# Chunked attention with a fused feed-forward layer: g, the second queries and the first tiles in another order

## The chip, the cores and the metric

The kernel runs on one core of a Trainium2 chip. The metric is the device time of one execution in microseconds (us); a kernel's time is the median of several executions. The profile comes from one more execution, taken by the hardware profiler. TensorE (PE) multiplies matrices, VectorE (DVE) and ScalarE (ACT) work element by element, GpSimd (POOL) and SyncE (SP) mainly issue transfers (DMAs) here; POOL also does some small arithmetic.

## The reference

Attention in chunks, with a few memory keys and values for each head, and then a feed-forward layer on the result:

```python
B, H, S, D = 4, 8, 768, 64        # chunk 32, left context 16, right context 8, 8 memory keys
for c in range(S // 32):
    q_c = q[:, :, 32*c : 32*c + 32]
    k_ctx, v_ctx = k, v at positions max(0, 32*c - 16) to min(S, 32*c + 40)
    k_full, v_full = concat(mem_k, k_ctx), concat(mem_v, v_ctx)
    a = softmax(q_c @ k_full.T / sqrt(D))
    attn[:, :, 32*c : 32*c + 32] = a @ v_full
x  = attn.transpose(0, 2, 1, 3).reshape(B, S, 512)
xn = (x - mean(x)) / sqrt(var(x) + 1e-6) * g_ln
out = x + max(xn @ w_ch1, 0) @ w_ch2          # w_ch1 512 x 2048, w_ch2 2048 x 512
```

All inputs and the output are float32; the kernel multiplies in float16.

## The kernel before

**Tiles, groups and blocks.** A tile is 128 rows of the sequence of one batch entry; there are six for each of four entries, 24 in all. A group is 64 rows (two chunks) and has its own window of 104 key columns in `KT`: 16 keys to its left, 64 own, 8 to its right, 8 zero columns and 8 memory keys. Tile t works with groups 2t and 2t+1. A block is 256 rows, so four groups or two tiles: queries and keys are loaded a block at a time.

**From load to output.** Keys and queries arrive in `st` (the very first blocks in float32, in output buffers borrowed for it), are rearranged by a copy into `iv` (`mix`, `mix_raw`), turned by TensorE against an identity matrix (`transpose_block`, `first_q`), and copied from PSUM into `KT` (`window`, `pieces`, `key_left`, `key_right`) and `QR` (`part_q`, `whole_q`). For a tile, `scores` (line 289) makes 16 products into an `att` slot of PSUM, `soften` two exponentials on ACT, `values` (line 312) 16 products with `V` and then a reciprocal, a scaling and a mean on DVE; `norm` (line 335) subtracts the mean and multiplies by g, which `gb` holds on all 128 partitions; `turn_x` (line 356) turns the result into `xT`. The feed-forward layer takes W1 in four quarters `w1c` and W2 in four `w2c`. `up_tile(u, c, i)` (line 398) multiplies tile i of a group of three with quarter c of W1 (16 products) and clips below zero with `relu` into `rT`; `up` does the same for three tiles at once; `down` multiplies with W2 and adds up in PSUM, and `finish` scales, adds x and stores. V also needs rows for the memory values (`v_mem`), which come from `mem_v` by `mem_vals`.

**What sets the order.** The order is written out by hand, and each engine runs its own instructions in that order, waiting for what it needs. Lines 560 to 629 are the start: tiles 0 to 2 of the first batch entry, and the first up tiles, all written call by call. From line 630 on a plan (`at(u, step, ...)`) places calls beside steps of the feed-forward layer: u counts groups of three tiles, and in the first group steps 10 to 15 are the last six `up_tile` calls, from step 16 on `down`. PSUM has two `att` slots and four `mm` banks, each taken in turn by `slot`; one is free again when its reader on DVE or ACT is done. `warm(n)` (line 455) issues n products of a zero matrix with 512 columns that nobody reads.

**The transfers.** SP's queue loads the first keys and queries and small tensors (lines 469 to 485); POOL's queue (lines 510 to 552, then the plan) loads everything else in the order written, converting to float16 on the way. A transfer on POOL's queue is issued when the eighth one before it has landed.

**g before.** `moe_g_ln` is loaded into one row, `grow`; `spread_g` (line 556) multiplies it on TensorE with a row of ones, `gone`, in two halves, into the bank `mm[3]`, and DVE copies that to `gb` (line 585).

**The first 30 us as written.** After key block 0 and the first half of query block 0 come tile 0's scores, then the second query half with the second half of g, tile 0's values, the turn of key block 1 and ACT's copies of it with the right edge of group 3 (lines 591 to 594), tile 1's scores, first up tiles, the turn of the whole query block 1 (lines 611 to 613), tile 2's scores, and further up tiles. DVE's `mix(0, 2, 0)` (line 626) prepares key block 2, which `turn_keys` turns in step 12.

Of the kernel before, what the change touches and what calls it, by code (L numbers as in the profile page):

```python
# [8 lines left out]
FP32 = mybir.dt.float32  # L9
# [6 lines left out]
def kernel(  # L16
# [34 lines left out]
    memv16 = sb.tile([W, B, H, VW], FP16, name="memv16")  # L51
    memKT = sb.tile([128, B, 4, 8], FP16, name="memKT")
    gb = sb.tile([128, 512], FP32, name="gb")
    grow = sb.tile([1, 512], FP32, name="grow")
    gone = sb.tile([1, 128], FP32, name="gone")
    band = sb.tile([128, 2], FP32, name="band")
    cnt = sb.tile([128, 3], FP32, name="cnt")
    mhalf = sb.tile([128, 1], FP32, name="mhalf")
# [31 lines left out]
    def dram(t, offset, pattern):  # L90
        return bass.AP(tensor=t.tensor, offset=offset, ap=[list(p) for p in pattern])
# [17 lines left out]
    def pick(lst, key):  # L109
        key = (id(lst),) + key  # L110
        if key not in ring:
            ring[key] = ring.setdefault(("n", id(lst)), 0) % len(lst)
            ring[("n", id(lst))] += 1
        return lst[ring[key]]


    def load_block(b, blk, which):
        s = pick(st, ("b", b, blk, which))
        for par in range(2):
            nc.gpsimd.dma_start(  # L120
                out=s[:, 512 * par : 512 * par + 512],
                in_=dram((k, q)[which], (b * H + 4 * par) * HS + blk * 256 * D,
                         [[512, 32], [HS, 4], [1, 512]]),
            )

    def load_v(b, g):
        lo, hi = 16 if g == 0 else 0, 80 if g == NG - 1 else 96
        nc.gpsimd.dma_start(  # L128
            out=V[b % 2][lo:hi, g, :, 0:64],
            in_=dram(v, b * H * HS + (64 * g - 16 + lo) * D, [[64, hi - lo], [HS, H], [1, 64]]),  # L130
        )

    def v_mem(b, g0, g1, eng):
        src = memv16[96:W, b, :, :]
        copy(eng, free(V[b % 2][96:W, g0:g1, :, :], 0, [[H * VW, g1 - g0], [1, H * VW]]),
             bass.AP(tensor=src.tensor, offset=src.offset,
                     ap=[list(src.ap[0]), [0, g1 - g0], [1, H * VW]]))

    def load_w1(c):
        nc.gpsimd.dma_start(  # L140
            out=w1c[c], in_=dram(moe_w_ch1, 512 * c, [[FF, 128], [128 * FF, 4], [1, 512]])
        )
# [54 lines left out]
    def pieces(b, blk, banks, phase):  # L197

        for n in range(2):
            key_piece(b, banks[phase], 4 * blk + n, *PIECES[n], dve, phase)  # L200
            key_piece(b, banks[1 - phase], 4 * blk + 2 + n, *PIECES[2 + n], act, 1 - phase)

    def window(b, blk, banks, k0, eng):

        for half in ((0, 1) if eng is dve else (1, 0)):
            key_piece(b, banks[half], 4 * blk + k0, *PIECES[k0], eng, half)
# [45 lines left out]
    def mix_raw(which, srcs, half, eng, lo=0, hi=128):  # L252

        o = pick(iv, ("b", 0, 0, which))[lo:hi, :]
        r0, n = (0, 8) if half is None else (4 * half, 4)
        for par in range(2):
            copy(eng, free(o, 128 * r0 + 64 * par, [[128, n], [1, 64]]),
                 free(srcs[par][lo:hi, :], 64 * r0, [[64, n], [1, 64]]))

    def first_q(half):  # L260

        i = pick(iv, ("b", 0, 0, 1))
        rows = slice(64 * half, 64 * half + 64)
        for r in range(8):
            c = 128 * r + 64 * half
            nc.tensor.matmul(
                out=Q0[0][:, c : c + 64],
                lhsT=i[rows, 128 * r : 128 * r + 128], rhs=identity[rows, rows],
                is_transpose=True, start=True, stop=True, tile_position=(64 * half, 0),
            )  # L270

    def mix(b, blk, which, eng):
        s, o = pick(st, ("b", b, blk, which)), pick(iv, ("b", b, blk, which))
        copy(eng, free(o, 0, [[64, 2], [128, 8], [1, 64]]), s)
# [29 lines left out]
    def soften(b, t, c):  # L304
        p = score_slot[b, t]
        nc.scalar.activation(  # L306
            out=free(AT[t % 3], 32 * c, [[64, 16], [1, 32]]),
            in_=free(p, 4 * c, [[64, 16], [1, 4], [8, 8]], W),
            func=ACTF.Exp, bias=band[0:W, c : c + 1], scale=0.125,
        )  # L310
# [152 lines left out]
    def first_load(which, par, lo, hi, eng):  # L463
        eng.dma_start(
            out=raws[which][par][4 * lo : 4 * hi, :],
            in_=dram((k, q)[which], 4 * par * HS + 512 * lo, [[512, hi - lo], [HS, 4], [1, 512]]),
        )
# [3 lines left out]
    nc.sync.dma_start(out=memkf, in_=dram(mem_k, 0, [[512, 32], [1, 512]]))  # L471
    first_load(1, 0, 0, 16, nc.sync)
    first_load(1, 1, 0, 16, nc.gpsimd)
    nc.sync.dma_start(out=grow, in_=dram(moe_g_ln, 0, [[512, 1], [1, 512]]))

    nc.sync.dma_start(out=xs[5][96:W, :], in_=dram(mem_v, 0, [[64, 8], [512, 8], [1, 64]]))

    def load_mem_v():
        nc.gpsimd.dma_start(
            out=memv16[96:W, 1:B, :, 0:64].rearrange("p b h d -> p (b h) d"),  # L480
            in_=dram(mem_v, 4096, [[64, 8], [512, 24], [1, 64]]),
        )

    first_load(1, 0, 16, 32, nc.sync)
    first_load(1, 1, 16, 32, nc.sync)

    PAIR = 1.0 / 128 + 15.0 / 2**20

# [20 lines left out]
    ones(0, 0, 2, pool)  # L509
    load_block(0, 1, 0)  # L510
    nc.vector.memset(zero, 0.0)
    nc.vector.memset(gone, 1.0)
    clear_keys(0, dve)
    nc.vector.memset(mhalf, -0.5)
    nc.vector.memset(memv16.bitcast(FP32)[96:W, :, :, 32:40], PAIR)
# [11 lines left out]
    load_w1(0)  # L527
    load_v(0, 2)
    load_v(0, 3)
    load_w1(1)  # L530
    load_block(0, 1, 1)
    load_w1(2)
    load_v(0, 4)
    load_v(0, 5)
    load_w1(3)
    load_block(0, 2, 0)
    nc.gpsimd.memset(V[0][64:96, NG - 1, :, :], 0.0)
# [15 lines left out]

    K0 = [as16(mm[0]), as16(mm[1])]
    Q0 = [as16(mm[2]), as16(mm[3])]
    def spread_g(half):
        cols = slice(256 * half, 256 * half + 256)
        nc.tensor.matmul(out=mm[3][:, cols], lhsT=gone, rhs=grow[:, cols], start=True, stop=True)

    warm(10)  # L560
    mix_raw(0, raws[0], 0, dve)
    mix_raw(0, raws[0], 1, act)
# [3 lines left out]
    mem_keys()  # L566
    mix_raw(1, raws[1], 0, dve, 0, 64)
    mix_raw(1, raws[1], 1, act, 0, 64)
    first_q(0)
    window(0, 0, K0, 0, dve)  # L570
    window(0, 0, K0, 1, act)
    part_q(0, 0, 0, Q0[0], act)
    spread_g(0)
    memT()
    mem_cols(0, dve)
    scores(0, 0)
    mem_vals()
    soften(0, 0, 0)
    soften(0, 0, 1)
    mix_raw(1, raws[1], None, dve, 64, 128)  # L580
    v_mem(0, 0, 2, dve)
    mix(0, 1, 0, dve)
    spread_g(1)
    first_q(1)
    copy(dve, gb, mm[3])
    part_q(0, 0, 1, Q0[0], dve)
    values(0, 0)
    norm(0, 0)
    window(0, 0, K0, 2, act)
    window(0, 0, K0, 3, act)  # L590
    transpose_block(0, 1, 0, Q0)
    window(0, 1, Q0, 0, act)
    window(0, 1, Q0, 1, act)
    key_right(0, 3, act)
    warm(3, 512, mm[1])
    scores(0, 1)
    soften(0, 1, 0)
    soften(0, 1, 1)
    turn_x(0, 0)
    v_mem(0, 2, 4, dve)  # L600
    window(0, 1, Q0, 2, dve)
    window(0, 1, Q0, 3, act)
    key_left(0, 4, dve)
    turn["mm"] = 3
    up_tile(0, 0, 0, act)
    mix(0, 1, 1, act)
    values(0, 1)
    norm(0, 1)
    late = up_tile(0, 1, 0, None)
    turn_x(0, 1)  # L610
    Q1 = [as16(slot("mm")) for _ in range(2)]
    transpose_block(0, 1, 1, Q1)
    whole_q(0, 1, Q1)
    scores(0, 2)
    soften(0, 2, 0)
    soften(0, 2, 1)
    relu(dve, *late)
    v_mem(0, 4, 6, dve)
    up_tile(0, 0, 1, act)
    up_tile(0, 1, 1, dve)  # L620
    values(0, 2)
    norm(0, 2)
    up_tile(0, 2, 0, act)
    up_tile(0, 2, 1, act)
    turn_x(0, 2)
    mix(0, 2, 0, dve)
    total(cnt[:, 1:2], 0, 80)
    total(cnt[:, 2:3], 96, W)
# [7 lines left out]
    def attend(i, s0, s1, u):  # L636
# [11 lines left out]
        else:  # L648
            at(i // 3 - 1, (20, 22, 23)[i % 3], root, b, t)

    def root0(b, t):
        root(0, t)

    at(0, 12, turn_keys, 0, 2)
    at(0, 12, more_keys, 0, 2)
    at(0, 14, mix, 0, 2, 1, dve)
# [124 lines left out]
```

## Time and profile before

| | us |
|---|---|
| median of 8 runs | 224.27 |
| lowest and highest | 223.04, 224.83 |
| the profiled execution's own time | 224.55 |
| its span, first to last instruction | 222.8 |
| TensorE busy in it | 213.1 (96%) |
| VectorE, ScalarE, GpSimd busy | 134.5, 102.9, 99.0 |

Four views of the profile are used. The 40 slices show, for each engine, the busy share of a slice in tenths (9 is 90% or more); PEclk is the share of TensorE's clock that was granted, in tenths, and DMA the busy share of the 16 DMA engines. A table of stretches gives busy microseconds of PE, PEld (weight loads), DVE, ACT and POOL, with the number of instructions in brackets, then the granted clock, the DMA share and GB/s. The waits say which instruction's line waited for which, with the total in us, the count and the longest. A row of the timeline has the start, the duration, the engine, the line, the operation and what it writes and reads, and in brackets the idle time ahead of it and what ended that. L12 is line 12 of the kernel. Products are pipelined, so their durations can overlap.

### The profile page before, as it was taken

How to read it: one execution, taken by the hardware profiler on the slowest of the kernel's cores; microseconds unless marked ns; L12 is line 12 of the kernel's file. 1: busy time of each engine (PE TensorE's matmuls, PEld its weight loads, DVE VectorE, ACT ScalarE, POOL GpSimd, SP SyncE). 2: the span in 40 equal slices, each digit the busy share in tenths (PEclk: the TensorE clock that was granted, in tenths of full speed). 3: DMA queues.
4: the chain of work that ended last, by engine and by line, in shares of the span. 5: the costliest groups of instructions: out<-in, count | busy, mean ns of one | idle time of the engine just before them, and what ended most of it. 6: DMA issues, size and time to landing. Idle time of an engine off the chain costs nothing.

```text
span 222.8 us, 5004 instructions
## 1 busy us (share of the span) xinstructions
PE 213.1 (96%) x1974; PEld 131.6 (59%) x1974; DVE 134.5 (60%) x329; ACT 102.9 (46%) x217; POOL 99.0 (44%) x171
## 2 busy tenths in 40 slices
PE   7786979999999999999999999999999999999993
PEld 2566977547765566546664567446654666456553
DVE  4868456588879768834675678716845367234221
ACT  2755449525784246732791067424851365103200
POOL 7955695899598992212923793300021011100000
PEclk9759699999999999999999999999999999999999
DMA  6999999999969999277995799585112201211012
GB/s 167 185 193 193 199 194 204 171 143 192 163 98 165 172 183 164 46 165 188 133 161 93 101 159 183 59 192 129 26 24 74 94 15 35 71 57 40 0 47 94
DMA packets 72273, 27.70 MB, mean 124 GB/s; under 512 B 60345, under 2 KB 68281, under 8 KB 72250
## 3 DMA queue, kind: packets, MB, share of 16 engines
q0 software_dynamic: 46080, 14.71, 63.2%
q1 hardware_dynamic: 26026, 12.41, 24.3%
q8 instruction: 15, 0.25, 0.4%
q10 hardware_dynamic: 144, 0.26, 0.4%
q14 instruction: 8, 0.07, 0.1%
HBM read 30.28 MB, written 6.29 MB: 164 GB/s over the span
## 4 chain that ended last, share of the span: by engine, by line
PE 79%; DMA 13%; POOL 5%; issue 1%; DVE 0%; DVEq 0%; POOLq 0%
PE mm L420 34%; PE mm L391 34%; DMA w1c<-in_moe_w_ch_dram 8%; PE att L296 5%; DMA st<-in_k_dram 5%; PE att L317 3%; POOL V L128 2%; PE mm L442 2%; POOL w2c L145 1%; POOL st L120 1%; PE att L218 1%; PE mm L218 1%; POOL V L491 0%; PE att L365 0%; POOL V L548 0%
## 5 line engine op out<-in xcount | busy, mean ns | idle before, releaser
L420 PE MATMUL mm<-w2c,rT 128*128 128x512 f16 x368 | 83.0, 379 | 0.0
L391 PE MATMUL mm<-xT,w1c 128*128 128x384 f16 x448 | 78.5, 327 | 0.0
L391 PEld LDWEIGHTS <-w1c 128*128 128x128 f16 x448 | 49.1, 114 | 22.1
L420 PEld LDWEIGHTS <-rT 128*128 128x128 f16 x368 | 34.9, 98 | 39.4
L385 DVE TENSOR_SCALAR rT<-mm 128x384 f16<-128x384 f32 (+1 forms) x61 | 34.3, 567 | 26.9 <-PE mm L391 21.7
L383 ACT ACTIVATE rT<-mm 128x384 f16<-128x384 f32 (+1 forms) x63 | 31.6, 506 | 40.8 <-PE mm L391 23.4
L306 ACT ACTIVATE AT<-att,band 104x512 f16<-104x512 f32 x48 | 31.3, 686 | 29.3 <-PE att L296 29.3
L128 POOL DMA_DIRECT2D V<-in_v_dram x48 | 39.5, 834 | 5.9 <-DMA w1c<-in_moe_w_ch_dram 3.9
L429 DVE SCALAR_TENSOR_TENSOR osb<-mm,rstd,xs 128x512 f32<-128x512 f32 x23 | 17.2, 749 | 33.6 <-PE mm L420 24.7
L348 POOL TENSOR_SCALAR veps<-sq 128x1 f32<-128x1 f32 x24 | 7.4, 309 | 66.3 <-ACT junk L342 52.8
L342 ACT ACTIVATE junk<-xs,nmean 128x512 f16<-128x512 f32 x24 | 17.4, 726 | 15.1 <-DVE nmean L331 13.2
L337 DVE SCALAR_TENSOR_TENSOR xn<-xs,nmean,gb 128x512 f16<-128x512 f32 x24 | 18.0, 748 | 0.4
L296 PE MATMUL att<-QR,KT 64*104 64x64 f16 x384 | 16.0, 235 | 1.2 <-ACT QR L102 1.1
L325 DVE SCALAR_TENSOR_TENSOR xs<-att,rec 128x512 f32<-128x512 f32 x24 | 16.6, 692 | 0.8
L296 PEld LDWEIGHTS <-KT 64*104 64x104 f16 x384 | 12.9, 135 | 5.7 <-issue 3.8
L352 POOL TENSOR_TENSOR rstd<-veps,mhalf 128x1 f32<-128x1 f32 x24 | 14.6, 610 | 2.0
L402 PE MATMUL mm<-xT,w1c 128*128 128x128 f16 x192 | 13.3, 233 | 1.5 <-DVE xT L370 1.5
L120 POOL DMA_DIRECT2D st<-in_k_dram x22 | 13.4, 639 | 2.0 <-DVE KT L104 2.0
L120 POOL DMA_DIRECT2D st<-in_q_dram x22 | 12.6, 595 | 3.0 <-DMA w2c<-in_moe_w_ch_dram 1.9
L402 PEld LDWEIGHTS <-w1c 128*128 128x128 f16 x192 | 12.3, 119 | 2.1 <-DVE xT L370 1.2
L317 PEld LDWEIGHTS <-AT 104*64 104x64 f16 x384 | 8.4, 114 | 7.3 <-issue 4.3
L102 ACT COPY KT<-rawk 128x352 f16<-128x352 f16 (+1 forms) x12 | 9.0, 814 | 5.7 <-DMA rawk<-iv 5.7
(78 smaller groups left out, 141.4 us busy)
## 6 DMA issues: line engine op xcount, KB each, us to landing
out_dram<-osb SPq DMA_DIRECT2D x23, 256.0 KB, 2.2
V<-in_v_dram POOLq DMA_DIRECT2D x40, 96.0 KB, 5.2
st<-in_k_dram POOLq DMA_DIRECT2D x22, 128.0 KB, 5.2
st<-in_q_dram POOLq DMA_DIRECT2D x22, 128.0 KB, 6.5
w1c<-in_moe_w_ch_dram POOLq DMA_DIRECT2D x4, 512.0 KB, 10.0
w2c<-in_moe_w_ch_dram POOLq DMA_DIRECT2D x4, 512.0 KB, 8.6
V<-in_v_dram POOLq DMA_DIRECT2D x8, 80.0 KB, 5.5
xT<-xn SPq DMA_TRANSPOSE x17, 2.4
```

The source lines that it names most:

```text
L120: nc.gpsimd.dma_start(out=s[:, 512 * par : 512 * par + 512], in_=dram((k, q)[which], (b * H + 4 * par) * HS + blk * 256 * D, [[512, 32], [ ...
L128: nc.gpsimd.dma_start(out=V[b % 2][lo:hi, g, :, 0:64], in_=dram(v, b * H * HS + (64 * g - 16 + lo) * D, [[64, hi - lo], [HS, H], [1, 64]]),)
L296: nc.tensor.matmul(out=p[0:W, par, (4 * gg + j) * 64 : (4 * gg + j) * 64 + 64], lhsT=KT[b % 2][rows, 2 * t + gg, j, :], rhs=free(QR[b % 2] ...
L306: nc.scalar.activation(out=free(AT[t % 3], 32 * c, [[64, 16], [1, 32]]), in_=free(p, 4 * c, [[64, 16], [1, 4], [8, 8]], W), func=ACTF.Exp, ...
L337: nc.vector.scalar_tensor_tensor(out=xn[i % 4], in0=xs[i % 9], scalar=nmean[t], in1=gb, op0=ALU.add, op1=ALU.mult,)
L342: nc.scalar.activation(out=junk, in_=xs[(NT * b + t) % 9], func=ACTF.Square, bias=nmean[t], scale=1.0, accum_out=sq[t],)
L383: nc.scalar.activation(out=o, in_=p, func=ACTF.Relu)
L385: nc.vector.tensor_scalar(out=o, in0=p, scalar1=0.0, scalar2=None, op0=ALU.max)
L391: nc.tensor.matmul(out=p, lhsT=free(w1c[c][:, dt, :], i, [[4, 128]]), rhs=xT[u % 2][:, dt, 128 * lo : 128 * (lo + n)], start=(dt == 0), st ...
L402: nc.tensor.matmul(out=p[:, 128 * k_ : 128 * k_ + 128], lhsT=free(w1c[c][:, dt, :], k_, [[4, 128]]), rhs=xT[u % 2][:, dt, 128 * i : 128 * ...
L420: nc.tensor.matmul(out=p, lhsT=rT[c][:, k_, 128 * i : 128 * i + 128], rhs=w2c[c][:, k_, :], start=(c == 0 and k_ == 0), stop=(c == 3 and k ...
L429: nc.vector.scalar_tensor_tensor(out=o, in0=p, scalar=rstd[t % 9], in1=xs[t % 9], op0=ALU.mult, op1=ALU.add,)
```

## The change

Three things change, and with them the order of the start.

- g comes to all 128 partitions by one transfer on SP's queue that reads the same row for each; `grow`, `gone`, `spread_g` and the copy fall away. The second half of the first queries is moved ahead of `mem_v` and g on that queue.
- Query block 1 is loaded, rearranged and turned in two halves of 64 partitions (`load_q`, `mix_q`, `half_q`). The half for tile 2 is loaded ahead of W1's quarter 1, and V's groups 4 and 5 ahead of quarter 2; the half for tile 3 is loaded ahead of quarter 3 and turned in step 11 of the plan (`late_q`).
- Key block 1 is turned ahead of tile 0's values. For tile 1's scores only its first eight keys are copied (`first_right`, on DVE); the other copies of block 1 follow tile 1's values.

More fillers (`warm`) stand between the calls: 13 in place of 3 after the first query half. Two up tiles change places, and some copies change engine. In the diff below, context is cut.

```diff
     memv16 = sb.tile([W, B, H, VW], FP16, name="memv16")
     memKT = sb.tile([128, B, 4, 8], FP16, name="memKT")
     gb = sb.tile([128, 512], FP32, name="gb")
-    grow = sb.tile([1, 512], FP32, name="grow")
-    gone = sb.tile([1, 128], FP32, name="gone")
     band = sb.tile([128, 2], FP32, name="band")
     cnt = sb.tile([128, 3], FP32, name="cnt")
     mhalf = sb.tile([128, 1], FP32, name="mhalf")
...
             key_piece(b, banks[phase], 4 * blk + n, *PIECES[n], dve, phase)
             key_piece(b, banks[1 - phase], 4 * blk + 2 + n, *PIECES[2 + n], act, 1 - phase)
 
+    def first_right(b, g, banks):
+
+        for half in range(2):
+            copy(dve, free(KT[b % 2], GW * g + 80 + 4 * half, [[W, 4], [1, 4]]),
+                 free(banks[half], 0, [[1, 4], [128, 4]]))
+
     def window(b, blk, banks, k0, eng):
 
         for half in ((0, 1) if eng is dve else (1, 0)):
...
             copy(eng, free(o, 128 * r0 + 64 * par, [[128, n], [1, 64]]),
                  free(srcs[par][lo:hi, :], 64 * r0, [[64, n], [1, 64]]))
 
-    def first_q(half):
-
-        i = pick(iv, ("b", 0, 0, 1))
+    def load_q(b, blk, half):
+        s = pick(st, ("b", b, blk, 1))[64 * half : 64 * half + 64, :]
+        for par in range(2):
+            nc.gpsimd.dma_start(
+                out=s[:, 512 * par : 512 * par + 512],
+                in_=dram(q, (b * H + 4 * par) * HS + (blk * 256 + 128 * half) * D,
+                         [[512, 16], [HS, 4], [1, 512]]),
+            )
+
+    def mix_q(b, blk, half, eng):
+        rows = slice(64 * half, 64 * half + 64)
+        s, o = pick(st, ("b", b, blk, 1))[rows, :], pick(iv, ("b", b, blk, 1))[rows, :]
+        copy(eng, free(o, 0, [[64, 2], [128, 8], [1, 64]]), s)
+
+    def half_q(b, blk, half, pv):
+
+        i = pick(iv, ("b", b, blk, 1))
         rows = slice(64 * half, 64 * half + 64)
         for r in range(8):
             c = 128 * r + 64 * half
             nc.tensor.matmul(
-                out=Q0[0][:, c : c + 64],
+                out=pv[:, c : c + 64],
                 lhsT=i[rows, 128 * r : 128 * r + 128], rhs=identity[rows, rows],
                 is_transpose=True, start=True, stop=True, tile_position=(64 * half, 0),
             )
...
     nc.sync.dma_start(out=memkf, in_=dram(mem_k, 0, [[512, 32], [1, 512]]))
     first_load(1, 0, 0, 16, nc.sync)
     first_load(1, 1, 0, 16, nc.gpsimd)
-    nc.sync.dma_start(out=grow, in_=dram(moe_g_ln, 0, [[512, 1], [1, 512]]))
-
+    first_load(1, 0, 16, 32, nc.sync)
+    first_load(1, 1, 16, 32, nc.sync)
     nc.sync.dma_start(out=xs[5][96:W, :], in_=dram(mem_v, 0, [[64, 8], [512, 8], [1, 64]]))
+    nc.sync.dma_start(out=gb, in_=dram(moe_g_ln, 0, [[0, 128], [1, 512]]))
 
     def load_mem_v():
         nc.gpsimd.dma_start(
             out=memv16[96:W, 1:B, :, 0:64].rearrange("p b h d -> p (b h) d"),
             in_=dram(mem_v, 4096, [[64, 8], [512, 24], [1, 64]]),
         )
-
-    first_load(1, 0, 16, 32, nc.sync)
-    first_load(1, 1, 16, 32, nc.sync)
 
     PAIR = 1.0 / 128 + 15.0 / 2**20
 
...
     ones(0, 0, 2, pool)
     load_block(0, 1, 0)
     nc.vector.memset(zero, 0.0)
-    nc.vector.memset(gone, 1.0)
     clear_keys(0, dve)
     nc.vector.memset(mhalf, -0.5)
     nc.vector.memset(memv16.bitcast(FP32)[96:W, :, :, 32:40], PAIR)
...
     load_w1(0)
     load_v(0, 2)
     load_v(0, 3)
+    load_q(0, 1, 0)
     load_w1(1)
-    load_block(0, 1, 1)
-    load_w1(2)
     load_v(0, 4)
     load_v(0, 5)
+    load_w1(2)
+    load_q(0, 1, 1)
     load_w1(3)
     load_block(0, 2, 0)
     nc.gpsimd.memset(V[0][64:96, NG - 1, :, :], 0.0)
...
 
     K0 = [as16(mm[0]), as16(mm[1])]
     Q0 = [as16(mm[2]), as16(mm[3])]
-    def spread_g(half):
-        cols = slice(256 * half, 256 * half + 256)
-        nc.tensor.matmul(out=mm[3][:, cols], lhsT=gone, rhs=grow[:, cols], start=True, stop=True)
-
     warm(10)
     mix_raw(0, raws[0], 0, dve)
     mix_raw(0, raws[0], 1, act)
...
     mem_keys()
     mix_raw(1, raws[1], 0, dve, 0, 64)
     mix_raw(1, raws[1], 1, act, 0, 64)
-    first_q(0)
+    half_q(0, 0, 0, Q0[0])
     window(0, 0, K0, 0, dve)
     window(0, 0, K0, 1, act)
     part_q(0, 0, 0, Q0[0], act)
-    spread_g(0)
+    warm(3)
     memT()
     mem_cols(0, dve)
     scores(0, 0)
     mem_vals()
     soften(0, 0, 0)
     soften(0, 0, 1)
+    mix(0, 1, 0, dve)
+    transpose_block(0, 1, 0, Q0)
+    v_mem(0, 0, 2, dve)
     mix_raw(1, raws[1], None, dve, 64, 128)
-    v_mem(0, 0, 2, dve)
-    mix(0, 1, 0, dve)
-    spread_g(1)
-    first_q(1)
-    copy(dve, gb, mm[3])
-    part_q(0, 0, 1, Q0[0], dve)
+    warm(2, 512, att[1][:, 0, :])
+    half_q(0, 0, 1, as16(att[1][:, 1, :]))
+    first_right(0, 3, Q0)
+    part_q(0, 0, 1, as16(att[1][:, 1, :]), dve)
+    v_mem(0, 2, 4, dve)
     values(0, 0)
     norm(0, 0)
     window(0, 0, K0, 2, act)
     window(0, 0, K0, 3, act)
-    transpose_block(0, 1, 0, Q0)
-    window(0, 1, Q0, 0, act)
-    window(0, 1, Q0, 1, act)
-    key_right(0, 3, act)
-    warm(3, 512, mm[1])
+    warm(2, 512, att[0][:, 1, :])
     scores(0, 1)
     soften(0, 1, 0)
     soften(0, 1, 1)
+    warm(4, 512, mm[1])
     turn_x(0, 0)
-    v_mem(0, 2, 4, dve)
+    values(0, 1)
+    norm(0, 1)
+    window(0, 1, Q0, 0, act)
+    window(0, 1, Q0, 1, act)
+    key_left(0, 4, dve)
+    turn["mm"] = 3
+    late = up_tile(0, 0, 0, None)
+    mix_q(0, 1, 0, act)
+    warm(2, 512, mm[1])
+    Q1 = as16(slot("mm"))
+    half_q(0, 1, 0, Q1)
+    part_q(0, 1, 0, Q1, act)
     window(0, 1, Q0, 2, dve)
     window(0, 1, Q0, 3, act)
-    key_left(0, 4, dve)
-    turn["mm"] = 3
-    up_tile(0, 0, 0, act)
-    mix(0, 1, 1, act)
-    values(0, 1)
-    norm(0, 1)
-    late = up_tile(0, 1, 0, None)
     turn_x(0, 1)
-    Q1 = [as16(slot("mm")) for _ in range(2)]
-    transpose_block(0, 1, 1, Q1)
-    whole_q(0, 1, Q1)
     scores(0, 2)
     soften(0, 2, 0)
     soften(0, 2, 1)
     relu(dve, *late)
     v_mem(0, 4, 6, dve)
+    up_tile(0, 1, 0, act)
     up_tile(0, 0, 1, act)
-    up_tile(0, 1, 1, dve)
     values(0, 2)
     norm(0, 2)
+    up_tile(0, 1, 1, act)
     up_tile(0, 2, 0, act)
+    turn_x(0, 2)
     up_tile(0, 2, 1, act)
-    turn_x(0, 2)
+    mix_q(0, 1, 1, dve)
     mix(0, 2, 0, dve)
     total(cnt[:, 1:2], 0, 80)
     total(cnt[:, 2:3], 96, W)
...
         else:
             at(i // 3 - 1, (20, 22, 23)[i % 3], root, b, t)
 
+    def late_q():
+        pv = as16(slot("att")[:, 0, :])
+        half_q(0, 1, 1, pv)
+        part_q(0, 1, 1, pv, act)
+
     def root0(b, t):
         root(0, t)
 
+    at(0, 11, late_q)
     at(0, 12, turn_keys, 0, 2)
     at(0, 12, more_keys, 0, 2)
     at(0, 14, mix, 0, 2, 1, dve)
```

## The prediction

> **What bounds the kernel now.** I read the page first, its 40 slices.
>
> ```profile
> PE   7786979999999999999999999999999999999993
> ...
> PEclk9759699999999999999999999999999999999999
> DMA  6999999999969999277995799585112201211012
> ```
>
> A slice is 5.6 us. From the seventh on TensorE is full to the end, so what is saved there is only what TensorE need not do. Ahead of it, in the first 30 us, it has gaps and a lowered clock, and the DMA engines are full from the second slice. The change touches this start only, so I asked for a table of stretches, cut where the granted clock changes (every 3.41 us).
>
> ```profile
> 5.41:8.82 3.41, 2.39 (x36) 1.41 (x35) 3.01 (x10) 2.18 (x7) 3.41 (x6) 1.00 1.43 190
> 8.82:12.24 3.42, 3.12 (x42) 2.41 (x43) 2.92 (x7) 2.92 (x8) 2.90 (x4) 0.50 1.40 176
> 12.24:15.65 3.41, 3.26 (x31) 2.11 (x30) 1.93 (x6) 1.04 (x6) 1.78 (x3) 0.50 1.55 199
> 15.65:19.06 3.41, 2.74 (x52) 2.35 (x50) 2.65 (x9) 2.56 (x6) 1.39 (x3) 1.00 1.24 201
> 19.06:22.48 3.42, 1.80 (x35) 1.68 (x36) 2.76 (x6) 1.56 (x3) 2.40 (x5) 1.00 1.67 187
> 22.48:25.89 3.41, 3.41 (x45) 3.19 (x42) 0.43 (x1) 1.59 (x3) 1.44 (x3) 0.50 1.58 189
> 25.89:29.30 3.41, 2.42 (x41) 2.05 (x36) 2.33 (x7) 1.19 (x2) 3.33 (x6) 1.00 1.22 207
> ```
>
> After the length come busy us of PE, weight loads, DVE, ACT and POOL, then the clock. The idle stretch 19.06:22.48 (PE 1.80) is followed by one at half clock that is packed with up tiles: those cost 1.7 us more than at full clock. Next, who made TensorE wait (4 to 40 us), and the timeline rows around it.
>
> ```profile
> PE mm L402 <- DVE xT L370: 1.5, 2, 1.0
> PE att L296 <- ACT QR L102: 1.1, 2, 0.7
> PE att L365 <- DVE xn L337: 1.1, 1, 1.1
> ```
>
> ```profile
> 20.00 0.40 PE L365 MATMUL att<-identity,xn 128*128 128x128 f16 x4 [1.10 <-DVE xn L337]
> ...
> 21.52 0.65 PE L296 MATMUL att<-QR,KT 64*104 64x64 f16 x16 [0.68 <-ACT QR L102]
> ...
> 29.31 0.72 DVE L104 COPY iv<-st 128x1024 f16<-128x1024 f16 x1
> ...
> 32.16 0.61 PE L218 MATMUL mm<-identity,iv 128*128 128x128 f16 x8
> ```
>
> The third score product (tile 2) starts at 21.52, behind tile 1's normalisation and the second query block. 32.16 is the turn of key block 2: from there the order of TensorE's work is nearly the old one. I sum up to that point; TensorE is full after it, so a shift there is a shift of the end.
>
> **DMA order.** Times from issue to landing, asked for issue by issue, give landings: W1's quarter 0 at 13.6, V3 14.8, quarter 1 17.6, second queries 18.6, quarter 2 21.3, V4 22.0, V5 22.5, quarter 3 25.0, key block 2 26.3. The differences are prices in a full queue: 2.9 for quarter 1, 1.0 for both query transfers, 2.6 for quarter 2, 0.7 and 0.6 for V4 and V5.
>
> The spread of g now is 256 KB on SP's queue. The hardware queue's row of the first 40 us
>
> ```profile
> q1 hardware_dynamic: 506, 0.74, 6.5%
> ```
>
> is 2.6 us of all 16 engines for 0.74 MB, so 0.9 us for 0.26 MB. Bounds: nothing, if it finds room; 1.3 us at the 200 GB/s of the table; no row has 128 reads of one 2 KB row, so more is possible (first rival). I take 0.9. It then puts off everything that lands after about 11 us: quarter 0 14.5, V3 15.7. The query half (half of 1.0) lands at 16.2, quarter 1 19.1, V5 20.4, quarter 2 23.0, key block 2 27.2. g itself should land near 11; its first reader, tile 0's normalisation, comes at 14.6 below. mem_v moves behind two query loads, which cost about 0.9 us each (6.83, 8.78, 9.71 are their landings): its reader on ACT stood at 9.09 without a wait and may move to 9.7. That holds the first exponential 0 to 0.4 us; I take nothing, as 0.35 us idle stands ahead of that exponential now.
>
> POOL issues two transfers more at 0.55 us each; in the stretches above it has idle time up to 2 us, and each transfer waits for the eighth before it anyway (V5 waited 1.99 us for quarter 0), so nothing. The Trainium skill (DMA: Bandwidth & Descriptors, "Rules for kernel authors") speaks against the split: two transfers to disjoint partition halves serialise, use one. Its fixed 2 us for a transfer ("Anatomy of one DMA") would make the two more transfers up to 4 us of queue, key block 2 would land at 31, and the gain would be gone. The rows say that in this full queue V5 lands 0.6 us after V4: the fixed part overlaps. I go by the rows; the split then only brings half of the queries before quarter 1.
>
> **TensorE up to tile 2's scores.** Nothing changes up to 8.06. Out go two one-row products of 0.69 us (7.99) and two of 1.22 (9.95), and DVE's copy of g, 0.69 (11.36). The three fillers at 8.0 (0.65) lie in the wait for the queries that ends at 9.12: free. The memset of the ones (0.17 at 1.08) went before DVE's wait of 0.72 for the identity: nothing.
>
> Then, at half clock by the rows above: tile 0's scores 9.12 to 10.0. The turn of key block 1, whose mix DVE now does first (8.93 to 9.4), costs 0.9: 10.9. Two fillers of 0.43: 11.8. The second query half's turn 0.5: 12.3; its casts on DVE are done by 11.4.
>
> DVE's copy of it, 0.45: 12.75. Behind it tile 0's values, which share its PSUM tile: 13.4 (now 11.63 to 12.28, so 1.1 later). Behind that copy DVE holds the memory values of groups 2 and 3 (0.49) and then tile 0's reciprocal; they lie under the products, and without that cover the norm comes 0.5 later. Two fillers: 14.25. Tile 1's scores, which no longer wait for ACT's four copies of block 1 and the right edge (13.48 to 14.48): 14.25 to 15.15, 0.4 earlier.
>
> Four fillers to 16.3 (clock up at 15.65). Tile 0's norm ends on DVE at 15.4, so the turn of its xn comes at 16.3, 0.8 later than now; xT at 17.1 (now 16.4).
>
> ACT: tile 1's exponentials to 16.5; copies of block 1, 0.9, to 17.4; mix of the query half, 1.04 as its row now, to 18.45 (landed 16.2).
>
> TensorE: tile 1's values 16.65 (now 17.45; V3 15.7), up tile 17.1 to 18.1, two fillers to 18.5, turn of the query half to 18.9. ACT's copy 0.6: 19.5. Tile 2's scores 19.55 to 20.2: 2.0 earlier than 21.52. DVE ends tile 1's norm at 19.0, and xT of tile 1, behind the moved key copies, at 20.2.
>
> **From there to the turn of key block 2.** 8 up tiles of 0.95 (1.98 for two, 2.7 for three in the timeline), 7.6; tile 2's values 0.4; the turn of its xn 0.4 and 0.1 wait; the late query half 0.45: 8.95, so 29.15. Quarter 1 (19.1) and quarter 2 (23.0, used at 23.5) are there. Now this takes 22.10 to 32.16 with one up tile and the query half less, because of 1.7 us of clock and a wait of 1.0.
>
> One wait is new. DVE mixes key block 2 as it lands: now at 29.31, 3 us after landing, then at 27.2. Queued behind it on DVE are three sums (0.45) and the relu of the first up tile of tile 2, whose bank the turn needs: 27.2+0.5+0.45+0.7 = 28.9. Just inside 29.15. The mix of the second query half stands ahead of it on DVE; its data land near 23.5 and DVE comes to it at 25.4, so it waits for nothing. So 32.16−29.15 = 3.0 us gained.
>
> **Does it last?** Later transfers land 0.9 later and are wanted 3.0 earlier. W2's quarter 1 lands at 35.6 and is used at 40.2; quarter 2 39.2 and 44.5; quarter 3 41.7 and 47.8: 0.7 us and more stay. Block 2's queries (31.4, mixed at 35.23) and the next batch's first keys (43.2, mixed at 46.95) come out even. So it lasts, barely.
>
> The profiled execution has 224.55, a span of 222.8 and 1.75 around it. 224.55−3.0 = 221.55. The median is 0.28 lower: 221.3 to 221.5, I say 221.4.
>
> **The clock.** Leaving out turns and one-row products, the stretches held 0.55 (then down), 1.5 (stayed down), 2.44 (up), 2.58 (stayed), 1.03 (down), 3.4 (up), 2.1 (stayed). The changed ones would hold: 8.82:12.24 1.76, taken as still low; 12.24:15.65 about 2.8, up; 15.65:19.06 2.4, stays; 19.06:22.48 2.5, stays. So the fall at 22.48 goes. The skill (TensorE: Matmul & The Clock Gate, "Why this matters for your kernels") asks only for no idle gap over about 3 us. Here none is over 1.1 us, yet the clock fell twice. By the rule the fillers are useless and 1.7 of the 3.0 us couldn't come from them (222.9 to 223.1); by the rows it is the busy share of a stretch that counts, and I use that.
>
> **Rivals.**
> Slower: key block 2 comes late into DVE's queue. From a landing of about 27.4 on, each us goes through the mix, the sums and the relu to TensorE one for one; at 30.5 nothing is left, at 31.3 it is slower by 0.3%. The spread of g would have to cost 5 us instead of 0.9, say because 128 reads of one row queue up. At 5.2 us (landing 31.5, turn 33.15, 1.0 later than now): 225.3. For it: DMA is the full resource and no row shows such a read. Against: other loads on that queue pay 0.9. Chance 0.09.
>
> The clock falls once more, at 19.06, or rises one stretch late: half clock for 3.4 us, 1.7 us lost, 222.3 to 223.2. For it: my count of 2.4 is near the lowest that stayed (2.1). Chance 0.17.
>
> It doesn't bring tile 2 forward: values of tile 0 come 1.1 later, the query half passes ACT in line behind other copies, and the longer chain eats what the scores gain. About 1 us from the clock, less 0.9 of DMA: 223.7 to 224.8, no change. Chance 0.08.
>
> More than forecast: the spread of g rides free and the clock rises at 12.24. Then key block 2 allows about 28.0: 220.3. Chance 0.10.
>
> The forecast, 220.7 to 222.3: 0.56.
>
> Faster by over 0.3% (about what a measurement can tell): 0.56+0.17+0.10 = 0.83; within 0.08; slower 0.09. The range 220.0 to 223.3 leaves out the no-change and the slower case, 0.17, and a sliver of the others.
>
> **What would show it.** Right: tile 1's scores near 14.3, tile 2's near 19.6, no half clock after 15.65, the turn of key block 2 near 29.2 with DVE's mix waiting for its load, TensorE full after it. Wrong: g landing after 14.6 and tile 0's norm waiting on it; half clock in 19:26; TensorE idle on W1 or W2; gaps at 36 to 48.

## The result, and the profile after

The changed kernel takes 222.58 us (median of 11 runs, 221.62 to 223.48); its ratio to the kernel before is 0.9925, 95% interval 0.9906 to 0.9945. Forecast was 2.9 us less, measured are 1.7. The profiled execution has 223.01, a span of 221.2 and 1.8 around it, so it stands 0.4 above the median. Each ratio leaves out executions about 1.5% or more above the fastest of the same kernel, of which three of the experiments below have one each; a median is over all of them.

The 40 slices of the profile after:

```profile
PE   7779999999999999999999999999999999999993
...
PEclk9985999999999999999999999999999999999999
DMA  6999999999999999978994899594112211210012
```

TensorE is now full from the fourth slice instead of the seventh (in the fourth mostly at half clock), and one dip of the clock is left, in the third and fourth. The DMA engines are full longer, to the sixteenth. The stretches of the kernel after, cut where its own clock changes:

```profile
4.46:7.88 3.42, 2.45 (x37) 1.33 (x36) 2.30 (x9) 1.57 (x5) 3.42 (x5) 1.00 1.15 197
7.88:11.29 3.41, 2.63 (x37) 1.56 (x35) 2.62 (x9) 3.29 (x10) 2.38 (x4) 1.00 1.21 158
11.29:14.70 3.41, 2.09 (x37) 1.26 (x37) 2.23 (x7) 0.57 (x3) 1.56 (x2) 1.00 1.64 187
14.70:18.12 3.42, 2.83 (x29) 1.93 (x28) 1.30 (x4) 2.40 (x7) 2.15 (x4) 0.50 1.50 193
18.12:21.53 3.41, 3.28 (x30) 2.24 (x29) 2.18 (x8) 1.05 (x4) 2.38 (x5) 0.50 1.50 194
21.53:24.94 3.41, 3.41 (x75) 3.20 (x75) 1.96 (x5) 2.62 (x6) 2.31 (x4) 1.00 1.24 204
```

The half clock (0.50 in the last column but two) that lay over 22.48:25.89 is gone; the one that should end at 15.65 lies over 14.70 to 21.53. Who made TensorE wait, 4 to 40 us, the two longest:

```profile
PE att L335 <- DVE V L102: 1.0, 1, 1.0
PE att L335 <- DMA V<-in_v_dram: 0.9, 3, 0.3
```

Before, TensorE waited for xT, xn and the queries; of these waits at most 0.3 us is left. Now its longest are ahead of the values products (L335): for DVE's copy of the memory values into V, which ended at 12.26, and for V's loads. V0 landed at 12.2, so the two came together; in the kernel with query block 1 loaded whole, below, the same wait (0.94) ends with V0's load. The timeline rows of TensorE around them:

```profile
12.29 0.19 PE L335 MATMUL att<-V,AT 104*64 104x65 f16 x1 [1.02 <-DVE V L102]
12.80 0.41 PE L335 MATMUL att<-V,AT 104*64 104x65 f16 x15 [0.32 <-DMA V<-in_v_dram]
...
13.68 0.64 PE L314 MATMUL att<-QR,KT 64*104 64x64 f16 x16
...
17.51 1.90 PE L420 MATMUL mm<-xT,w1c 128*128 128x128 f16 x16
19.20 1.06 PE L476 MATMUL mm<-zero 128*128 128x512 f16 x2
...
21.46 0.66 PE L314 MATMUL att<-QR,KT 64*104 64x64 f16 x16
...
30.72 0.61 PE L222 MATMUL mm<-identity,iv 128*128 128x128 f16 x8
```

Tile 1's scores start at 13.68 (before 14.66), but tile 2's at 21.46 (before 21.52): between them an up tile took 1.90 and two fillers 1.06 at half clock, instead of the 1.08 and 0.59 that they take at full clock (rows of the kernel with fillers in the wait, below). The turn of key block 2 is at 30.72, 1.44 earlier than before. The span is 1.6 shorter, so the shift did reach the end.

The loads: V0 was issued at 4.21 and took 8.0 us to land (5.7 before), so it landed at 12.2 instead of 9.9. Key block 2 landed at 28.1 (20.05 and 8.1) instead of 26.3. The hardware queue's row of the first 40 us:

```profile
q1 hardware_dynamic: 648, 1.00, 9.9%
```

Against 506 packets, 0.74 MB and 6.5% before, the spread of g added 0.26 MB, and 3.4% in time of packets, 1.4 us of all engines.

### The profile page after: what moved, and what is told of

It is laid out like the page before. It is cut to its first block, busy times and chain, and to the rows that moved or that the text cites. A ratio compares the mean times of both kernels' runs of the same rounds, so it can differ in the third digit from the quotient of the medians.

```text
span 221.2 us, 5037 instructions
## 1 busy us (share of the span) xinstructions
PE 212.5 (96%) x1988; PEld 130.5 (59%) x1988; DVE 132.8 (60%) x328; ACT 103.6 (47%) x218; POOL 98.8 (45%) x173
## 3 DMA queue, kind: packets, MB, share of 16 engines
q1 hardware_dynamic: 26168, 12.67, 26.3%
## 4 chain that ended last, share of the span: by engine, by line
PE 80%; DVE 0%; issue 0%; DVEq 0%
PE mm L438 34%; PE mm L409 34%; PE att L314 5%; PE att L335 3%; PE mm L460 2%; PE att L222 1%; PE mm L222 1%; PE att L383 0%; DVE osb L465 0%; DVEq L465 0%
## 5 line engine op out<-in xcount | busy, mean ns | idle before, releaser
L409 PEld LDWEIGHTS <-w1c 128*128 128x128 f16 x448 | 49.1, 114 | 22.0
L401 ACT ACTIVATE rT<-mm 128x384 f16<-128x384 f32 (+1 forms) x64 | 32.1, 505 | 36.2 <-PE mm L409 22.3
L403 DVE TENSOR_SCALAR rT<-mm 128x384 f16<-128x384 f32 (+1 forms) x60 | 33.6, 565 | 23.4 <-PE mm L409 22.0
L126 POOL DMA_DIRECT2D V<-in_v_dram x48 | 38.2, 803 | 9.9 <-DMA V<-in_v_dram 5.5
L360 ACT ACTIVATE junk<-xs,nmean 128x512 f16<-128x512 f32 x24 | 17.4, 723 | 15.1 <-DVE nmean L349 13.2
L314 PE MATMUL att<-QR,KT 64*104 64x64 f16 x384 | 15.5, 232 | 0.5 <-ACT QR L100 0.3
L314 PEld LDWEIGHTS <-KT 64*104 64x104 f16 x384 | 12.4, 129 | 4.7 <-issue 3.2
L335 PEld LDWEIGHTS <-AT 104*64 104x64 f16 x384 | 8.5, 112 | 9.3 <-issue 5.3
L335 PE MATMUL att<-V,AT 104*64 104x65 f16 x384 | 11.2, 200 | 2.1 <-DVE V L102 1.0
L342 DVE RECIPROCAL rec<-att 128x8 f32<-128x8 f32 x24 | 5.0, 207 | 13.7 <-PE att L335 13.3
L118 POOL DMA_DIRECT2D st<-in_q_dram x20 | 11.8, 612 | 2.3 <-DMA w2c<-in_moe_w_ch_dram 1.6
L420 PE MATMUL mm<-xT,w1c 128*128 128x128 f16 x192 | 12.8, 227 | 0.0
```

Source lines behind the costliest of these rows:

```text
L118: nc.gpsimd.dma_start(out=s[:, 512 * par : 512 * par + 512], in_=dram((k, q)[which], (b * H + 4 * par) * HS + blk * 256 * D, [[512, 32], [ ...
L126: nc.gpsimd.dma_start(out=V[b % 2][lo:hi, g, :, 0:64], in_=dram(v, b * H * HS + (64 * g - 16 + lo) * D, [[64, hi - lo], [HS, H], [1, 64]]),)
L314: nc.tensor.matmul(out=p[0:W, par, (4 * gg + j) * 64 : (4 * gg + j) * 64 + 64], lhsT=KT[b % 2][rows, 2 * t + gg, j, :], rhs=free(QR[b % 2] ...
L335: nc.tensor.matmul(out=p[64 * gg : 64 * gg + 64, par, 128 * j : 128 * j + HD], lhsT=AT[t % 3][:, par, gg, j, :], rhs=V[b % 2][:, 2 * t + g ...
L360: nc.scalar.activation(out=junk, in_=xs[(NT * b + t) % 9], func=ACTF.Square, bias=nmean[t], scale=1.0, accum_out=sq[t],)
L401: nc.scalar.activation(out=o, in_=p, func=ACTF.Relu)
```

## Experiments

Two theories stood at the start. The load theory: the spread of g by a transfer cost the loads more than my 0.9 us, and that is the missing gain. The clock theory: what is missing is the half clock between 14.7 and 21.5, whatever the loads do. Each number below is a median, with its ratio to the kernel before.

**No load of g at all.**

```diff
-    nc.sync.dma_start(out=gb, in_=dram(moe_g_ln, 0, [[0, 128], [1, 512]]))
+    nc.vector.memset(gb, 1.0)
```

> The changed kernel without any load of g: g is set to one on VectorE at the start, so the product with g is left out in effect. Load theory (the spread of g by a transfer put V0 to V3 and W1's quarter 0 off by 1.8 to 2.6 us, and that is what was lost against the forecast): V0 lands near 9.9 again, tile 0's values start near 11.8 instead of 12.3 to 12.8, tile 2's scores near 20.0 and the time is 221.0 to 221.6, 1.0 to 1.5 us below the changed kernel. Clock theory (the loss is the half clock from 14.7 to 21.5, which comes from too few fillers whatever the loads do): half clock in the same place and 222.3 to 222.8.

Measured: 220.67, ratio 0.9859 (0.9812 to 0.9906), so 1.9 below the changed kernel. V0 landed in 5.0 us, at 9.2, key block 2 at 25.6, 2.5 us earlier than with the transfer; tile 2's scores started at 19.60. Of the two stretches at half clock one is left in its profile, from 14.0 to 17.4. The load theory holds here, and more than it expected (221.0 to 221.6), but the clock moved along with it, so this run alone doesn't part the two.

**The kernel before, with g by the transfer alone.** The edit is the first part of the diff, with the transfer last on SP's queue.

> The kernel before with one part of the change alone: g by the transfer to all partitions, last on SP's queue, without the one-row products and without the copy. Load theory: V0 to V3 land 2 us later, tile 0's values wait for V0 to about 12.3 instead of 11.6, key block 2 lands 1 us later; 0.5 to 1.0 us slower than before, 224.8 to 225.3. Clock theory: the loads have slack, and TensorE loses only work in waits: within 0.3 us of before.

Measured: 225.29, ratio 1.0057 (1.003 to 1.0083): 1.1 slower. V0 landed at 11.9, key block 2 at 28.3, 2.0 us later than before. The time is as the load theory had it, the landing twice as late as it had it (1 us). This part of the change costs, alone, more than it spares TensorE.

**Fewer fillers.**

```diff
-    warm(2, 512, att[1][:, 0, :])
...
-    warm(2, 512, att[0][:, 1, :])
...
-    warm(4, 512, mm[1])
...
-    warm(2, 512, mm[1])
```

> The changed kernel without its ten fillers after the turn of key block 1 (the three at 8 us stay). Clock theory: the busy share of the stretches sinks, half clock lasts from about 11 to past 22, and up tiles run in it: 223.3 to 224.3. Load theory: the fillers stand in waits and do nothing, 222.3 to 222.8, or up to 0.8 us faster because two of them ran at half clock in line ahead of the second queries (19.2 to 20.25).

Measured: 224.05, ratio 1.0005 (0.9986 to 1.0024): without these ten fillers nothing of the gain is left. The stretches of its profile, cut where its clock changes:

```profile
5.39:8.80 3.41, 2.58 (x37) 1.33 (x36) 2.75 (x11) 2.15 (x7) 3.41 (x6) 1.00 1.09 195
8.80:12.22 3.42, 1.66 (x34) 1.43 (x34) 2.54 (x9) 2.94 (x8) 1.35 (x3) 1.00 1.27 170
12.22:15.63 3.41, 1.98 (x36) 1.64 (x36) 2.19 (x6) 1.56 (x5) 1.82 (x3) 0.50 1.67 186
15.63:19.05 3.42, 3.03 (x40) 2.48 (x38) 2.20 (x7) 1.51 (x4) 2.79 (x5) 0.50 1.56 191
19.05:22.46 3.41, 3.28 (x42) 3.02 (x40) 2.13 (x7) 2.24 (x5) 2.59 (x4) 0.50 1.38 199
22.46:25.87 3.41, 3.41 (x45) 3.15 (x43) 0.68 (x2) 1.19 (x2) 1.87 (x4) 0.50 1.28 202
```

A stretch with TensorE busy for 1.66 us is followed by half clock in four stretches, up to 25.87, with up tiles in them. So the clock is worth 1.5 us here, and the load theory alone is not enough.

**Fillers in the wait itself.**

```diff
+    warm(5, 512, att[0][:, 1, :])
     values(0, 0)
     norm(0, 0)
...
-    warm(2, 512, att[0][:, 1, :])
```

> The changed kernel with five fillers ahead of tile 0's values, in the wait for V0, in place of the two behind them. Clock theory: the stretch with the wait of 1.0 us is filled, the clock stays up through 14.7 or comes back earlier, up tile and fillers at 17.5 to 20.2 run at full clock: 221.2 to 221.8. Load theory: V0 and V1 still land at 12.2 and 12.8, nothing else moves, 222.3 to 222.8.

Measured: 222.87, ratio 0.9942 (0.9918 to 0.9966), no faster than the change, though the granted clock of its profile is 1.00 throughout and tile 2's scores start at 19.39. Both theories miss. The time is close to the load theory's 222.3 to 222.8, but its "nothing else moves" is not so: the clock was won and the time was not. Where it went stands in DVE's rows:

```profile
28.79 0.74 DVE L102 COPY iv<-st 128x1024 f16<-128x1024 f16 x1 [2.85 <-DMA st<-in_k_dram]
29.46 0.28 DVE L515 TENSOR_REDUCE cnt<-identity 128x1 f32<-128x80 f16 x2
29.78 0.16 DVE L643 TENSOR_TENSOR cnt<-cnt 128x1 f32<-128x1 f32 x1
29.86 0.69 DVE L403 TENSOR_SCALAR rT<-mm 128x512 f16<-128x512 f32 x1
```

and in TensorE's:

```profile
29.59 0.62 PE L222 MATMUL mm<-identity,iv 128*128 128x128 f16 x8 [0.66 <-ACT rT L401]
30.61 1.95 PE L420 MATMUL mm<-xT,w1c 128*128 128x128 f16 x32 [0.39 <-DVE rT L403]
```

DVE stands 2.85 us in its mix until key block 2 lands, at 28.7, and the relu behind it holds up TensorE. From here I worked with a third theory of two limits: TensorE's chain, longer by its half clock, and the landing of key block 2; in the changed kernel both end near 30.

**g by products again, as it was.** Two one-row products in place of the two fillers after key block 1, copied by ScalarE. The diff leaves out the load of the row, which stands ahead of the second query half on SP's queue.

```diff
-    warm(2, 512, att[1][:, 0, :])
+    for half in range(2):
+        cols = slice(256 * half, 256 * half + 256)
+        nc.tensor.matmul(out=att[1][:, 0, cols], lhsT=gone, rhs=grow[:, cols], start=True, stop=True)
+    copy(act, gb, att[1][:, 0, :])
```

> The changed kernel with g spread as before: a load of one row and two one-row products, now in place of the two fillers after the turn of key block 1, and ScalarE's copy to all partitions after tile 0's exponentials. Load theory: V0 lands near 9.5, key block 2 near 25.6, and the time is that of the kernel without g's load, 220.4 to 221.2, so the spread by transfer is the part of the change that costs. If the one-row products don't count for the clock, half clock comes earlier than there and part is lost: 221.2 to 222.

Measured: 222.25, ratio 0.9907 (0.988 to 0.9933). Key block 2 landed at 25.4, but the turn of the second query half waited 0.67 us for ScalarE's copy, and the stretch with the products was followed by half clock:

```profile
6.82:10.23 3.41, 2.90 (x53) 1.87 (x51) 2.86 (x10) 2.42 (x7) 3.39 (x6) 1.00 1.59 197
10.23:13.64 3.41, 2.15 (x36) 1.55 (x33) 2.23 (x7) 2.57 (x7) 2.46 (x4) 1.00 1.68 185
13.64:17.06 3.42, 3.42 (x34) 1.54 (x27) 2.06 (x6) 1.39 (x4) 2.29 (x4) 0.50 1.56 194
```

The loads were better and the start longer, near the second of the two cases expected (221.2 to 222). With the products moved into the wait ahead of tile 0's values and the copy behind ScalarE's key copies it was no better:

> The changed kernel with g spread by two one-row products again, now in TensorE's wait ahead of tile 0's values, into the PSUM tile that tile 1's scores take next, and copied by ScalarE behind its key copies; two more fillers in that wait. Two-limit theory (the end hangs on the later of two things: TensorE's own chain, longer where a stretch runs at half clock, and VectorE's mix of key block 2, which the transfer of g puts off by 2.5 us): key block 2 lands near 25.5 and the wait is filled, so both limits go: 220.3 to 221.2. If the one-row products leave the stretch too idle for the clock: 221.2 to 222.2, as with the copy in the way (222.25).

Measured: 222.40, ratio 0.9911 (0.9878 to 0.9944).

**g on GpSimd's queue**, in line behind V0 and V1.

> The changed kernel with the same transfer of g on GpSimd's queue, in line behind V0 and V1, instead of beside them on SP's queue. If its price is its bytes (262 KB at 190 GB/s, 1.4 us), V0 and V1 land near 9.5 and 10, quarter 0 and all behind it 1.3 to 1.5 us later than without g, key block 2 near 27.0: 221.4 to 222.0. If it is the alternation of its 2 KB packets with the 128-byte packets of V0 and V1 on each engine that costs, most of the 2.5 us goes and key block 2 lands near 26.4: 220.9 to 221.5. If 128 reads of one row are slow in themselves, it stands before quarter 0 for 2.5 us: 222.5.

Measured: 222.62, ratio 0.994 (0.9914 to 0.9966). V0 and V1 landed at 9.9 and 10.4 and tile 0's values no longer waited for them; key block 2 still landed at 28.0. So the place in the queue moves which load is late first, not the sum, and neither of the two cheap prices holds; its 222.62 is as expected for the dear one.

**The other two parts undone, one each.** Query block 1 loaded whole (`load_block(0, 1, 1)` ahead of quarter 1, its second half's load left out):

> The changed kernel with query block 1 loaded whole ahead of W1's quarter 1 (its rearranging and turns stay in halves). The queries of tile 2 land 0.5 us later, and all loads from quarter 1 to quarter 2 too. By the order of loads: 0.3 to 0.6 us slower than the changed kernel, 222.8 to 223.2. If tile 2's queries aren't what the stage waits for (they landed at 17.3 and were used at 17.4 by ScalarE, but TensorE was then busy to 20.2): 222.4 to 222.8, no change.

Tile 1's scores behind all of ScalarE's copies of key block 1:

> The changed kernel with tile 1's scores again behind ScalarE's four copies of key block 1 and the right edge of group 3, as before, instead of the eight keys alone. If the eight keys help: the copies run on ScalarE from 11.5 to 12.4 while it would idle, and the scores (13.7) hardly wait: 222.4 to 222.8, no change, since tile 0's values with V0 come first on TensorE anyway. If tile 1's scores are what the stage hangs on: 0.5 to 1.0 us slower, 223.0 to 223.6.

Measured: 222.66, ratio 0.9944 (0.9921 to 0.9966), and 222.71, ratio 0.9936 (0.9914 to 0.9959). Neither can be told from the change as a whole. Beside the late loads both parts are worth nothing that is seen; what they would be worth without them was not tried.

**Key block 2 ahead of W1's quarter 3**, with the five fillers in the wait and without them.

```diff
+    load_block(0, 2, 0)
     load_w1(3)
-    load_block(0, 2, 0)
```

> The changed kernel with five fillers in the wait ahead of tile 0's values (alone 222.87, the full clock held and key block 2 late) and key block 2 loaded ahead of W1's quarter 3; g still by its transfer. Two-limit theory: key block 2 lands near 26.2 and quarter 3 near 28.7, used at 29.6; turn of key block 2 near 28.6, tile 3's scores near 31.0: 220.7 to 221.6. If late loads don't limit: 222.5 to 223.0.

> The changed kernel with key block 2 loaded ahead of W1's quarter 3 and nothing else. Two-limit theory: where a stretch runs at half clock TensorE's own chain ends last (turn at 30.7 in the profile, mix at 28.9), so little is gained: 221.9 to 222.5. If the late keys alone are the limit: 220.7 to 221.6. If W1's quarter 3 becomes late: 222.6 to 223.2.

Measured: 222.53, ratio 0.9924 (0.9896 to 0.9952), and 222.43, ratio 0.9932 (0.9904 to 0.996). The second is as expected, the first misses. In it key block 2 now landed at 26.2, but TensorE reached its turn only at 29.41, and most of what tile 3's scores gained (31.74 against 32.48 with the fillers alone) was given back later. DVE's and TensorE's rows of the first of the two:

```profile
44.91 0.73 DVE L102 COPY iv<-st 128x1024 f16<-128x1024 f16 x1 [0.58 <-DMA st<-in_k_dram]
```

```profile
46.69 0.40 PE L383 MATMUL att<-identity,xn 128*128 128x128 f16 x4 [0.65 <-DVE xn L355]
```

The next load is the limit, the first keys of the second batch entry: DVE waits for them with the last norm queued behind, and TensorE waits 0.65 us for that. So it isn't one late load: with key block 2 out of the way, the next one holds up TensorE.

**g in one float16 product.** If the loads must be spared and the clock held, g's spread has to use neither much of the DMA engines nor products of several passes (two float32 products show as four in the trace). The two rows, `grow` and `gone`, are float16 here; the diff leaves out the lines that fall away, the load of g to all partitions among them.

```diff
+    nc.gpsimd.dma_start(out=grow, in_=dram(moe_g_ln, 0, [[512, 1], [1, 512]]))
     load_v(0, 0)
...
+    window(0, 0, K0, 2, act)
+    window(0, 0, K0, 3, act)
+    nc.tensor.matmul(out=att[0][:, 0, :], lhsT=gone, rhs=grow, start=True, stop=True)
+    copy(act, gb, att[0][:, 0, :])
+    warm(4, 512, mm[1])
```

> The changed kernel with g spread by TensorE again, but in one 512-column product of float16 rows in the wait ahead of tile 0's values (g is rounded to float16 by its load, which is one row on GpSimd's queue), with ScalarE's copy behind its key copies and four fillers in that wait in place of the two behind the values. Theory of loads and clock: without the transfer V0 lands near 10 and key block 2 near 25.5, and with fillers that count the full clock holds through the start: tile 3's scores near 31.0, 220.3 to 221.2, as fast as the kernel without any load of g (220.67) or faster. If leaving out the transfer helps only by what TensorE is spared, or if the start is lengthened by the copy as in the two other kernels with a product (222.25, 222.4): 221.8 to 222.6.

Measured: 220.69, ratio 0.9851 (0.9829 to 0.9872), all five runs between 220.36 and 221.44: faster than the kernel before and than the change. The product is a single one in the trace:

```profile
11.49 0.39 PE L603 MATMUL att<-grow,gone 1*128 1x512 f16 x1
11.80 1.04 PE L478 MATMUL mm<-zero 128*128 128x512 f16 x4
12.77 0.44 PE L337 MATMUL att<-V,AT 104*64 104x65 f16 x16
...
18.75 0.65 PE L316 MATMUL att<-QR,KT 64*104 64x64 f16 x16
...
27.99 0.61 PE L224 MATMUL mm<-identity,iv 128*128 128x128 f16 x8
```

The clock is 1.00 throughout in its profile, V0 landed at 9.2, tile 2's scores start at 18.75 and key block 2 turns at 27.99, 2.7 us earlier than in the change. Not all went as expected: key block 2 landed at 26.7, not 25.5, so that DVE waited 1.61 us for it, and the first keys of the second batch entry still cost TensorE 0.55 us at 45.1.

## Why the prediction came out as it did

**The direction and the second half of the sum were right.** From tile 2's scores to the turn of key block 2 I had 9.6 us (19.55 to 29.15); the profile has 9.26 (21.46 to 30.72), at full clock from 21.53. The fall of the clock at 22.48 is gone, as expected, and a shift at that turn is a shift of the end: 1.44 there, 1.6 in the span.

**The step that failed is a term: "0.9 us for 0.26 MB".** In its place the runs show 2.0 to 2.5 us: key block 2 landed 2.0 us later with the transfer (the kernel before with the transfer alone) and 2.5 earlier without it. That is outside my bounds, 0 to 1.3; only the first rival left room for it. The way to the term was wrong. I took the time of the packets on SP's queue for a price. But the row of GpSimd's queue in the same view of the kernel before,

```profile
q0 software_dynamic: 13115, 6.58, 121.9%
```

makes 128% together with SP's 6.5%, so the times of packets overlap and a share of them is no share of the engines. By bytes it is more: the core moved 7.64 MB in those 40 us, 191 GB/s, and at that rate 0.26 MB take 1.4 us. And from 6 to 14 us, around the transfer, the core moved 179 GB/s with it and 195 without, 128 KB less or 0.7 us (176 against 186, 80 KB or 0.4 us, in the kernel before). That makes 2.1 of the 2.5 us and 1.8 of the 2.0. Why the rate sank stays open, and so does whether reading one row 128 times is slow in itself; no run read 128 different rows.

**Two steps hung on that term.** I had put off only what lands after about 11 us. V0 and V1, due before that, landed at 12.2 and 12.8, 2.3 and 2.6 later than before, and tile 0's values waited. And key block 2, due at "27.2", landed at 28.1 to 28.7, so that, with the transfer, the wait called new is a limit when the clock is held (222.87). "So it lasts, barely" was right in kind: the loads are what the start hangs on, and with 2 us more on them it lasts less.

**The clock.** I had half clock for two stretches, 8.82 to 15.65. The profiled execution has two as well, but later, over an up tile: the wait for V0 fell into the stretch 11.29 to 14.70, which held 2.09 us of TensorE, and half clock followed to 21.53. My count of filled time was not the right measure. I left turns out; counted so, 4.46:7.88 held 1.0 us and full clock stayed, 11.29:14.70 held 2.09 and it fell. With turns counted the order is right here (2.45 and 2.09), but not everywhere: with query block 1 loaded whole, a stretch of 2.18 us was followed by full clock, and the next, again 2.18, by half clock. What exactly counts stays open. That fillers hold the clock is shown: ten fewer cost 1.5 us, and with five in the wait 13 of 14 executions had a mean granted clock of 0.997 or more. The Trainium skill's rule of a 3 us gap (TensorE: Matmul & The Clock Gate, "Why this matters for your kernels") would have let the clock stay up here too: TensorE's longest wait in that stretch was 1.02.

**Clock and loads, told apart by executions.** Every execution has a mean granted clock. One stretch at half clock lowers it by 0.008 (half of 3.41 us in 221): 0.985 stands for two, as in the profile after, 0.977 for three, as in the one before. Sorted by that, and by the median us:

| half stretches | none | one | two | three |
|---|---|---|---|---|
| before, as timed beside the first four experiments | | | 223.1 (8) | 224.2 (30) |
| changed kernel | | 222.3 (8) | 222.9 (4) | |
| ten fillers fewer | | | 222.8 (1) | 223.6 (6) |
| five fillers in the wait | 222.8 (13) | 223.1 (1) | | |
| no load of g | 219.8 (3) | 221.2 (1) | 222.5 (1) | |

In brackets is the number of executions; some of the kernel before and most with ten fillers fewer have four half stretches or more. Most of the gain of 1.7 us is clock: at two half stretches each, before and after are only 0.2 apart, though the stretches needn't lie in the same places. With the transfer even full clock doesn't bring the 221.4 that I forecast. Without it full clock gives 219.8, and a half stretch costs about 1.4 us; that row rests on five executions. So what was missing is the late loads, and the clock counts in full only once they come earlier.

**mem_v behind the query loads** cost nothing, as taken: its reader on ACT ran at 8.81 without a wait. **The split of the second queries** cost nothing and brought nothing (222.66 loaded whole).

**The rivals.** The first named the right mechanism at about half of its price: the transfer of g makes key block 2 late in DVE's queue, not by 5 us but by 2.0 to 2.5, which eats gain instead of turning it into a loss. The measured 222.58 lies in the range of the second, a stretch more at half clock (222.3 to 223.2); but with five fillers in the wait the time stays there at full clock too (222.8), so the clock alone did not hold it there. The gain from a g that rides free, the last rival, came in the kernel that doesn't load g at all.

## What to carry to other kernels

Where the DMA engines are full, price an added transfer by its bytes at the rate the core really moves, and take that for the least (1.4 us here, against 2.0 to 2.5 measured). Then follow every load behind it to its reader; an engine's spare time says little. Where two limits end close together, taking one away shows nothing: fillers alone gave 222.87 and earlier keys alone 222.43, and of the kernels that spread g only the one with earlier loads and a held clock gave 220.69. Put fillers into the wait that lets the clock fall. If float16 is enough for a row, as it was taken to be for g, one short product spreads it over the partitions more cheaply than a transfer beside a full queue did here.

## What the runs showed of the hardware

A one-row product of 512 columns in float16 took 0.39 us by itself; two of 256 columns in float32 took 1.13 and show as four in the trace. So the "x2" of the one-row products before is one product, not two; their times, 0.69 and 1.22, stand. Whether such float32 products hold the clock isn't settled: a stretch with 2.15 us of TensorE, 1.13 of it such products, was followed by half clock (222.25), but so was one of 2.18 without any (222.66).

The changes of the clock lie 3.41 us or a multiple of it apart, and in each execution elsewhere: at 8.82, 15.65, 22.48 and 25.89 us in the profile before, at 14.70 and 21.53 after, at 14.0 and 17.4 without g. A transfer of 0.26 MB beside full queues put key block 2 off by 2.0 to 2.5 us, on SP's queue as on GpSimd's (28.1 and 28.0, against 25.6 without it).
